# A gated mix of linear attention and a Mish layer on one core: more products by blocks, a packed 96-unit tile, and a new order of all steps

## The chip, the core and the metric

The kernel runs on one core of a Trainium2 chip. Its time is the device time in microseconds of a launch; a profile of one execution gives the span from its first to its last instruction. Engines: TensorE (PE; PEld is its weight load), VectorE (DVE), ScalarE (ACT), GpSimd (POOL) and SyncE (SP), which issues most transfers.

## The reference

All in float32. x has 2048 rows of 512; there are 32 heads of 16.

```python
qkv = (x @ wqkv)                                    # q, k, v: 32 heads of 16
pq, pk = q @ w_phi, k @ w_phi                       # per head, 16 x 16
phi_q = concat(softmax(pq), softmax(-pq))           # 32 features a head; phi_k likewise
kv, z = sum_s phi_k^T v, sum_s phi_k                # over all 2048 rows
o = (phi_q kv) / (phi_q z + 1e-6)
a = o @ wo                                          # 512 x 512
h = x @ w1 + b1                                     # 512 x 1376
b = (h * tanh(softplus(h))) @ w2                    # Mish, 1376 x 512
g = sigmoid(sum(x * gate_w))
out = g * a + (1 - g) * b
```

## The kernel before

**Number format.** Almost every product is made of fp32r matmuls of 128 rows by 128 columns by 512. Each operand is split into a high part (a copy rounded to fp32r, on ScalarE) and a low part (operand minus high part, on VectorE or GpSimd). A product is then three matmuls: high by high, high by low, low by high. In the names a last letter h or l is the high or low part (wkh, wkl, xh, xl).

**Start.** The per-head w_phi is laid out as block-diagonal tiles `bds` and multiplied into the key and query weights once ("fuse"): for the keys by `fuse`, 128x128 matmuls, one bank per row tile k of the weights; for the queries by `fuse_tiles`, which sets 64x64 matmuls on four corners of the array, two row tiles a call. The result is copied out (raw: wkr, wqr) and split (wkh, wkl, wqh, wql).

**Part A: 8 chunks of 256 rows.** A chunk makes keys k, queries q and values v for its two row tiles: `proj`, 12 matmuls each (3 parts by 4 row tiles of the weights). Chunks 2 to 5 (`FAST`) make keys and queries with seven block products instead of eight: `fast_ops` has s1 to s7, six matmuls each; bc, m7, ca and qa carry partial results between banks; `fast_operands` makes sums of blocks of x (sa) and splits them (sh, sl); `tops` makes the sums of weight blocks. Keys go through maximum, minimum (mx, mn), two differences (d0, d1), Exp (E), sums (S), reciprocals (rS) and a scaling (ml). kv multiplies feature maps and values; z adds the maps up over chunks (in memory for the first chunks, then in a tile). The queries are stored to memory (`pqd`).

**Part B: 4 blocks of 512 rows.** The hidden layer has 11 unit tiles. The tile that holds the last 96 units of the first 736 also holds the gate's column, and comes first. up makes a tile (12 matmuls), mi applies Mish, hi and lo split it, dn adds its product to the four output banks (12 matmuls: three for each row tile t). Beside this the queries are loaded (lq) and go the same way as the keys; T, D, m, de, rd, sc, es multiply by z, form the denominator and scale; tr transposes 32x32 squares; mv moves the squares into place by 16 transfers for two row tiles; nu multiplies by kv; oh, ol split; wo multiplies by wo; ag, fi mix with the gate and store the block.

**Order.** Every instruction keeps its place in program order on its engine. The order is written out by hand: one text for each chunk and block (FIRST to LAST, BLOCK0 to BLOCK), whose words name steps. A mark ' is the chunk before, + the one after, # a step on the weights: L loads a piece of w1 or w2, H and O split it (O on GpSimd, with an added dependency that puts it behind a VectorE step, `behind`). All pieces are loaded and split during part A. Buffers come in turn from pools: PSUM has 3 banks "a", 4 banks "dn" (output and scratch) and 1 bank "kv".

Of the kernel before, what the change touches and what calls it, by code (L numbers as in the profile page):

```python
# [39 lines left out]
FIRST = """  # L40
    fq v0 fh0 fh1 wr0 wr1 fh2 fh3 fl0 fl1 wr2 wr3 mx0 mn0 d00 d10 fl2 fl3 xh xl ldx ve0 E0 mx1 mn1 d01 d11 v1 t1# t3# t4# ve1 E1
    S0 rS0 ml0 S1 rS1 ml1 q0 qe0 st0 q1 qe1 st1
"""
SECOND = """
    L0# L1# h0# h1# sa ldx z0' z1' k0 mx0 mn0 d00 d10 k1 E0 xh mx1 mn1 d01 d11 v0 E1 S0 rS0 ve0 sh0 ml0 xl sl0 z0
    v1 S1 rS1 ml1 ve1 q0 qe0 st0 q1 qe1 st1 t2# sh1
"""
THIRD = """
    h3# l1# h2# l2# l3# v0 kk ve0 H0# xh xl sl1' z1' l0# s1 bc sa s7 m7 H1# s2 mx0 mn0 s6 ca d00 d10 E0 ldx sh0 sl0 v1 O0# L2# ve1
    S0 s5 qa rS0 s4 st1 mx1 mn1 d01 d11 s3 qe0 st0 ml0 O1# L3# z0  # L50
"""
FOURTH = """
    s1 bc E1' S1' rS1' ml1' ve1' s7 m7 sh1' s2 xh s6 ca xl z1' sl1' sa ldx H2# O2# L4# mx0 mn0 d00 d10 E0 v0 ve0 sh0 sl0 H3#
    s4 s5 qa st1 S0 rS0 mx1 mn1 d01 d11 v1 s3 qe0 st0 ml0 z0
"""
SEVEN = """
    s1 bc E1' S1' rS1' ml1' ve1' s7 m7 sh1' s2 kk xh xl z1' early zld sa more mx0 s6 ca mn0 d00 d10 E0 ldx v0 ve0 sh0 sl0 za rest S0 rS0
    s4 s5 qa st1 mx1 mn1 d01 d11 E1 ml0 late v1 S1 rS1 s3 ve1 qe0 st0 ml1
"""
NEXT = """  # L60
    lq0+ k0 xh xl O8# L6# mx0 mn0 k1 kk d00 d10 ldx H9# E0 O9# ldw0 L10# z0' mx1 mn1 d01 d11 H6# E1 S0 rS0 ml0 z1' v0 ve0
    S1 rS1 ml1 O6# ldw1 v1 ve1 q0 mx0+ mn0+ d00+ d10+ z0 z1 qe0 st0 q1 qe1 st1 H10# O10# E0+ lq1+
"""
LAST = """
    k0 mx0 mn0 d00 d10 k1 E0 XH0 kv' mx1 mn1 d01 d11 E1 v0 S0 rS0 ml0 z0 ve0 ldo XH1 mx1+ mn1+ S1 rS1 ml1 d01+ d11+
    XL0 XL1 z1 v1 ve1 E1+ lq2+ q0 WH0 qe0 st0 q1 WH1 qe1 st1 tb kv S0+ rS0+ km zh0 zl0 zh1 zl1
"""

BLOCK0 = """
    up0 mi0 hi0 lo0 gr lq3 S1 rS1 mx2 mn2 d02 d12 up1 @z mi1 hi1 lo1 T0 D0 m0 de0 rd0 sc0 es0 tr0 up2 mi2 hi2 lo2 WL0 dn0
    T1 D1 m1 de1 rd1 sc1 es1 tr1 mv0 lq0+ lq1+ mx3 mn3 d03 d13 up3 @kt mi3 hi3 lo3 WL1 dn1
    up4 mi4 hi4 lo4 dn2 E2 S2 T2 rS2 D2 m2 de2 rd2 sc2 es2 tr2 up5 mi5 hi5 lo5 dn3 E3 ge gg up6 mi6 hi6 lo6 dn4
    up7 mi7 hi7 lo7 dn5 nu0 oh0 S3 T3 rS3 ol0 D3 m3 de3 rd3 sc3 es3 tr3 mv1 up8 mi8 hi8 lo8 dn6
    mx0+ mn0+ d00+ d10+ mx1+ mn1+ d01+ d11+ lq2+ lq3+ wo0 ag0 wo1 ag1 E0+ E1+ S0+ T0+ rS0+ D0+ m0+ de0+ rd0+ sc0+ es0+ tr0+
    up9 mi9 hi9 lo9 dn7 up10 mi10 hi10 lo10 dn8 S1+ T1+ nu1 oh1 ol1 rS1+ D1+ LX0 LX1 m1+ de1+ rd1+ sc1+ es1+ tr1+ mv0+
    XH0+ XL0+ XH1+ XL1+ dn9 wo2 ag2 wo3 ag3 df0 fi0 df1 fi1 df2 fi2 df3 fi3
"""
BLOCK1 = """  # L80
    up0 mi0 hi0 lo0 gr mx2 mn2 d02 d12 mx3 mn3 d03 d13 up1 mi1 hi1 lo1 E2 E3 S2 T2 rS2 D2 m2 de2 rd2 sc2 es2 tr2
    up2 mi2 hi2 lo2 dn0 nu0 oh0 ol0 S3 T3 rS3 D3 m3 de3 rd3 sc3 es3 tr3 lq0+ lq1+ mv1 up3 mi3 hi3 lo3 dn1 up4 mi4 hi4 lo4 dn2
    mx0+ mn0+ d00+ d10+ mx1+ mn1+ d01+ d11+ lq2+ lq3+ up5 mi5 hi5 lo5 dn3 E0+ E1+ ge gg wo0 ag0 wo1 ag1
    S0+ T0+ rS0+ D0+ m0+ de0+ rd0+ sc0+ es0+ tr0+ up6 mi6 hi6 lo6 dn4 up7 mi7 hi7 lo7 dn5 nu1 oh1 ol1 S1+ T1+ rS1+ D1+ LX0 LX1
    m1+ de1+ rd1+ sc1+ es1+ tr1+ mv0+ mx2+ mn2+ d02+ d12+ mx3+ mn3+ d03+ d13+ up8 mi8 hi8 lo8 dn6 E2+ E3+
    wo2 ag2 wo3 ag3 up9 mi9 hi9 lo9 dn7 up10 mi10 hi10 lo10 dn8 XH0+ XL0+ XH1+ XL1+ dn9 df0 fi0 df1 fi1 df2 fi2 df3 fi3
"""
BLOCK = """
    up0 mi0 hi0 lo0 gr S2 T2 rS2 D2 m2 de2 rd2 sc2 es2 tr2 up1 mi1 hi1 lo1 up2 mi2 hi2 lo2 dn0 nu0 oh0 ol0
    S3 T3 rS3 D3 m3 de3 rd3 sc3 es3 tr3 lq0+ lq1+ mv1 up3 mi3 hi3 lo3 dn1 up4 mi4 hi4 lo4 dn2  # L90
    mx0+ mn0+ d00+ d10+ mx1+ mn1+ d01+ d11+ lq2+ lq3+ up5 mi5 hi5 lo5 dn3 E0+ E1+ ge gg wo0 ag0 wo1 ag1
    S0+ T0+ rS0+ D0+ m0+ de0+ rd0+ sc0+ es0+ tr0+ up6 mi6 hi6 lo6 dn4 nu1 oh1 ol1 S1+ T1+ rS1+ D1+ LX0 LX1 m1+ de1+ rd1+ sc1+
    es1+ tr1+ mv0+ up7 mi7 hi7 lo7 dn5 mx2+ mn2+ d02+ d12+ mx3+ mn3+ d03+ d13+ up8 mi8 hi8 lo8 dn6 E2+ E3+
    wo2 ag2 wo3 ag3 up9 mi9 hi9 lo9 dn7 up10 mi10 hi10 lo10 dn8 XH0+ XL0+ XH1+ XL1+ dn9 df0 fi0 df1 fi1 df2 fi2 df3 fi3
# [4 lines left out]
def tile_gated_mix(ctx: ExitStack, tc: tile.TileContext, xT, wv, wkT, wqT, bd, w1a, w1b, b1, w2a, w2b, wo, out):  # L99
# [100 lines left out]
    ge_sb = const.tile([P, S // P], F32, name="ge_sb")  # L200
# [17 lines left out]
    xs, Es, vs, psA, low = {}, {}, {}, {}, {}  # L218
# [38 lines left out]
    def x_lo(c, j, eng):  # L257
        low[c] = dve[0] = pin(eng.tensor_sub(xs[c][1][j], kt(rawx[c], SC)[:, 2 * j : 2 * j + 2, :], f32(xs[c][0][j])))

    def feat_ops(key, t, src, d, negative=False):  # L260

        n = str(t)

        def red(name, op):
            d[name] = T([P, H], F32, name, 2, name)
            pin(V.tensor_reduce(d[name], hv(src()), axis=AX.X, op=op))
# [12 lines left out]
        def ss():
            d["S"] = T([P, 2 * H], F32, "Sm", 2, "Sm")  # L280
            pin(V.tensor_reduce(d["S"], hv(d["E"][:, :]), axis=AX.X, op=ALU.add))  # L281
# [7 lines left out]
        at(key, "rS" + n, lambda: pin(V.reciprocal(d["S"], d["S"])))

    dve = {}

    def behind(ins, other=None):
        tc.add_manual_dep(ins.ins, (other or dve[0]).ins.name, SYNC, reason="VectorE's step first")

    def scale_by(d, eng):
        dve[0] = pin(eng.tensor_mul(hv(d["E"][:, :]), hv(d["E"][:, :]), d["S"][:, :, None].to_broadcast([P, 2 * H, DH])))  # L297

# [32 lines left out]
    def fast_operands(c, key):  # L331
# [12 lines left out]
        for j in range(2):  # L344
# [615 lines left out]
```

## Time and profile before

| | |
|---|---|
| median of 3 runs | 447.27 us (447.27 to 448.22) |
| span of the profiled execution | 446.1 us |
| TensorE busy | 439.7 us, 99% |
| VectorE busy | 319.6 us, 72% |
| ScalarE busy | 211.3 us, 47% |
| GpSimd busy | 158.9 us, 36% |
| transfers | 46.35 MB, mean 104 GB/s |

The profiled execution's own launch time is not listed; its span is 1.17 us under the median. A busy bar of a matmul overlaps that of the next, so the busy share of TensorE is not its rate: the rate is read from the distance between starts. L111 is the helper that records every matmul, so groups are told apart by their tiles (up, down, proj, num, kvp, wo, fuse).

### The profile page before, as it was taken

What the parts mean: (1) busy time and instruction counts of PE and PEld (TensorE: products, weight loads), DVE (VectorE), ACT (ScalarE), POOL (GpSimd) and SP (SyncE); (2) the same over time, 40 slices, a digit from 0 to 9 for tenths busy, and PEclk for the clock granted to TensorE, in tenths of its full rate; (3) what the DMA queues carried; (4) which work ended last, traced back from release to release, by engine and by line L of the source; (5) the groups of instructions that cost most, each with busy time, mean ns of one, the idle gap of its engine ahead of it and who ended that gap; (6) DMA issues with size and microseconds to landing.
All of it is one profiled execution on the core that took longest, in us unless ns stands there. A gap on an engine that the chain in (4) does not pass through costs nothing.

```text
span 446.1 us, 7022 instructions
## 1 busy us (share of the span) xinstructions
PE 439.7 (99%) x2748; PEld 359.1 (81%) x2748; DVE 319.6 (72%) x427; ACT 211.3 (47%) x292; POOL 158.9 (36%) x120
## 2 busy tenths in 40 slices
PE   7999999999999999999999999999999999999996
PEld 7888888788888888787878887887887888787885
DVE  2499789888999999799899868386967438701002
ACT  5774644463544837426374443724253544234220
POOL 2297388675666364212023121113202123121211
PEclk9999999999999999999999999999999999999999
DMA  7424559949835111405251241321241302030002
GB/s 281 169 77 160 143 122 233 220 130 312 240 116 166 49 24 32 112 19 148 89 171 49 55 134 48 94 96 47 49 143 48 94 2 95 1 91 5 0 0 94
DMA packets 27320, 46.35 MB, mean 104 GB/s; under 512 B 5908, under 2 KB 14100, under 8 KB 27288
## 3 DMA queue, kind: packets, MB, share of 16 engines
q1 hardware_dynamic: 25528, 39.88, 28.9%
q0 software_dynamic: 1616, 5.77, 6.5%
q8 instruction: 21, 0.34, 0.3%
q10 hardware_dynamic: 144, 0.26, 0.2%
q14 instruction: 11, 0.09, 0.1%
HBM read 23.87 MB, written 13.64 MB: 84 GB/s over the span
## 4 chain that ended last, share of the span: by engine, by line
PE 98%; DMA 1%; DVE 0%; issue 0%
PE proj L111 28%; PE up L111 27%; PE down L111 27%; PE wo L111 10%; PE num L111 2%; PE fuse L111 2%; PE kvp L111 2%; DMA bds<-in_bd_dram 1%; DVE io L797 0%; PE z L111 0%; PE kvT L616 0%
## 5 line engine op out<-in xcount | busy, mean ns | idle before, releaser
L662 POOL TENSOR_TENSOR l<-act,h 128x512 fp32r<-128x512 f32 x44 | 60.4, 1373 | 220.5 <-ACT h L131 184.7
L131 ACT ACTIVATE act<-up,b1s 128x512 f32<-128x512 f32 x44 | 30.3, 689 | 87.4 <-PE up L111 87.3
L131 ACT ACTIVATE E<-E 128x1024 f32<-128x1024 f32 x32 | 33.7, 1060 | 47.9 <-DVE E L275 33.8
L297 DVE TENSOR_TENSOR E<-E,Sm 128x1024 f32<-128x1024 f32 x32 | 42.2, 1320 | 1.0
L281 DVE TENSOR_REDUCE Sm<-E 128x64 f32<-128x1024 f32 x32 | 38.7, 1210 | 4.2 <-ACT E L131 4.2
L111 PE MATMUL wo<-woh,ohl 128*128 128x512 f32 x128 | 40.7, 389 | 0.0
L111 PE MATMUL down<-w2ah,h 128*128 128x512 f32 x96 | 37.5, 390 | 0.0
L111 PE MATMUL down<-w2ah,l 128*128 128x512 f32 x96 | 37.4, 389 | 0.0
L111 PE MATMUL down<-w2al,h 128*128 128x512 f32 x96 | 37.3, 389 | 0.0
L797 DVE SCALAR_TENSOR_TENSOR io<-down,og_sb,io 128x512 f32<-128x512 f32 x16 | 11.1, 748 | 31.0 <-PE down L111 31.0
L111 PE MATMUL down<-w2bh,h 128*128 128x512 f32 x80 | 31.2, 390 | 0.0
L111 PE MATMUL down<-w2bl,h 128*128 128x512 f32 x80 | 31.1, 389 | 0.0
L111 PE MATMUL down<-w2bh,l 128*128 128x512 f32 x80 | 31.1, 389 | 0.0
L131 ACT ACT_TABLE_LOAD x20 | 25.7, 1283 | 10.1 <-PE up L111 9.8
L771 DVE TENSOR_TENSOR ohl<-num,ohl 128x512 fp32r<-128x512 f32 x16 | 10.2, 678 | 26.4 <-ACT ohl L131 26.4
L131 ACT ACTIVATE h<-act 128x512 fp32r<-128x512 f32 x44 | 27.8, 632 | 1.4
L111 PEld LDWEIGHTS wo<-woh,ohl 128*128 128x128 f32 x128 | 24.0, 188 | 5.0
L111 PE MATMUL up<-xbh,w1ah 128*128 128x512 f32 x96 | 26.2, 394 | 0.0
L111 PE MATMUL up<-xbh,w1al 128*128 128x512 f32 x96 | 25.7, 389 | 0.0
L111 PE MATMUL up<-xbl,w1ah 128*128 128x512 f32 x96 | 25.7, 389 | 0.0
L559 DVE TENSOR_TENSOR xbl<-xraw,xbh 128x1024 fp32r<-128x1024 f32 x8 | 10.1, 1290 | 21.0 <-ACT xbh L131 21.0
L111 PE MATMUL wo<-wol,ohl 128*128 128x512 f32 x64 | 24.9, 389 | 0.0
(155 smaller groups left out, 1015.3 us busy)
## 6 DMA issues: line engine op xcount, KB each, us to landing
xraw<-in_xT_dram SPq DMA_DIRECT2D x16, 512.0 KB, 4.6
eT<-tt SPq DMA_DIRECT2D x128, 64.0 KB, 2.0
zd<-E POOLq DMA_DIRECT2D x10, 512.0 KB, 7.4
pqd<-qs SPq DMA_DIRECT2D x16, 256.0 KB, 4.0
pq<-pqd SPq DMA_DIRECT2D x16, 256.0 KB, 2.9
out_dram<-io SPq DMA_DIRECT2D x16, 256.0 KB, 2.1
raw<-in_w1a_dram SPq DMA_DIRECT2D x3, 512.0 KB, 4.2
raw<-in_w2a_dram SPq DMA_DIRECT2D x3, 512.0 KB, 3.6
```

Source lines behind the costliest of these rows:

```text
L111: return pin(nc.tensor.matmul(*a, **k))
L131: return pin(A_.activation(out_, in_, fn, **k))
L281: pin(V.tensor_reduce(d["S"], hv(d["E"][:, :]), axis=AX.X, op=ALU.add))
L297: dve[0] = pin(eng.tensor_mul(hv(d["E"][:, :]), hv(d["E"][:, :]), d["S"][:, :, None].to_broadcast([P, 2 * H, DH])))
L559: dve[0] = pin(V.tensor_sub(xb[b][1][:, :, sl], kt(raw[h], SC), f32(xb[b][0][:, :, sl])))
L662: pin(G_.tensor_sub(U[i]["l"], U[i]["a"], f32(U[i]["h"])))
L771: pin(V.tensor_sub(ohl[h, gp][:, 512:], num[h, gp], f32(ohl[h, gp][:, :512])))
L797: pin(V.scalar_tensor_tensor(io[t], dn[t], og_sb[:, i : i + 1], io[t], op0=ALU.mult, op1=ALU.add))
```

## The change

1. `FAST` is chunks 2 to 7: chunks 6 and 7 make keys and queries by seven block products too.
2. The key weights are fused by `fuse_tiles` as well; `fuse` is gone.
3. The first unit tile (96 units) has its low parts put into its 32 free rows: two matmuls for each row tile instead of three, and a step dc of four matmuls over 32 rows for the remaining 32 units' low parts. w2 gets matching rows (`w2_moves`, six transfers on GpSimd's queue).
4. The second parts of w1 and w2 (pieces 4, 5, 9, 10, 11) are loaded and split in the first block of part B.
5. Transposed feature maps go through memory: a store (st) and four loads (ld) for each row tile; the transpose is in place. In part B the reciprocals rS are gone: the sums of the other half are multiplied in instead.
6. One text `ORDER` of 44 lines replaces the texts for chunks and blocks. A word is a step; `A3:` names its chunk; `@` gives the buffer or bank by number; a last v or g puts the step on VectorE or GpSimd; `^` adds the dependency on the last VectorE step noted. dn steps are single row tiles (a to d).

```diff
-FAST = range(2, 6)
+FAST = range(2, 8)
+SUM = 5
...
+ORDER = """
+    P0| lk0 lk1 fk0@12 lx0@0 kh1 kl1 lk2 kh0 kl0 xh0 kr1 lk3 fk1@30 kr3 kr2 kr0 kh2 xl0v kl2 lx1 xh1 xl1g kh3 lq2 lq3 p00@0 p01@1 p10 fq1@21 qh3 p11 kl3 p21 p31 A0:mx1@0
+    P0| A0:d01@0 lq1 A0:mn1@0 A0:d11 ldx@1 A0:xh@4576 A0:xl1g^ qr2 qr3 p20 p30 A0:mx0@1 A0:mn0@1 A0:d10@1 A0:xl0g qh2 ql2 lq0 A0:E1 lv0@0 vh0 vl0g fq0@30 lv1@1 A0:ldx@0
...
+    A7| s6 ca@0 B0:LX0@1 B0:XH0 mx0@1 A6:rS0 B0:LX1@0 B0:lq0@1 v1@1 ve1@0 B0:XL0v A6:rS1 d10@2 s5 A6:ml1v s4 B0:XH1 B0:XL1v mn1@1 W:L3@0 W:H3 qa W:wm A6:v0@3 st1 d00
+    A7| v0@0 A6:ve0@1 mx1@0 E0 d11@3 d01 E1 S0@0 rS0 B0:up0@1 B0:mi0@4 B0:ha@5 s3 A6:ml0g^ A6:z0g qe0@0 A6:v1@1 st0 S1@1 ml0g^ rS1 B0:mx0@1 A6:ve1@2 B0:d00g@1 ve0@3
+    B0| A6:z1v A7:z0v A7:ml1v A7:z1v A7:zh0@10 up2@2 mi2@7 mn0@0 A6:kv A7:kv A7:km@1 hb@6 pi d10v up3@0 W:L4@1 A7:zl0v ph W:H4 W:O4v up1@2 dn0d@3 lq2@0 mi3@0 A7:zh1
+    B0| A7:zl1g mn2@1 A7:z0b@2 E0 d12g@0 dn0a@1 W:O3v lq1@1 mn1@0 A7:zc0 A7:z1b@0 h3@2 up4@0 l3g^@1 dn0b@2 mi1@3 mx2@0 W:L5@1 W:H5 W:O5g up7@2 up10@1 A7:zc1 dn0c@0
...
+    B0| dn2a lq3@1 S0@0 m0 dn2d de0 rd0 sc0 mn3@1 d13g^@3 E2 dn2c mi5@4 up6@0 S1@1 m1 de1 rd1 mx3@1 d03g^ B1:lq0@0 sc1 es0v tr0 es1v W:L9@1 tr1 dn2b B1:lq1@1 st0 up8@2
+    B0| T2g@0 st1 D2@0 S2@0 mi7@7 W:H10 W:O10g^ m2 h5@2 l5g@1 dn4b dn5b up9@0 de2 W:L11@0 B1:mx1@0 W:H9 W:O9g mi6@3 h6@0 rd2 mi10@4 sc2 dn5d l6v@5 dn6d E3 T3v@0 dn6abc
+    B0| dn5ac W:H11 h7@6 l7g@3 ld0 dc es2g^ A7:kc ld1 mi8@7 h8@0 W:O11v l8g@5 nu0@1 dn8b mi9@2 dn8c B1:mn0@0 dn8d B1:mn1@1 A7:ldo@1 h9@1 l9g@7 dn9cd S3@1 B1:XH0 dn9b
...
-    def fuse(staged, k):
-        acc = psum("fuse", "dn")
-        for G in range(NG):
-            mm(acc[:, G * P : (G + 1) * P], staged[:, k, G, :], bds[:, G, :], start=(G == 0), stop=(G == NG - 1), skip_group_check=True)
-        return acc
...
+        def down_mm(t, a, w):
+            n = left.setdefault(t, 3 * NF)
+            if n == 3 * NF:
+                dn[t] = psum("down", "dn")
+            left[t] -= 1
+            mm(dn[t], a, w, start=(n == 3 * NF), stop=(n == 1), skip_group_check=True)
 
         def down(i, t):
...
-            for n, (a, x) in enumerate(((h, 0), (h, 1), (l, 0))):
-                mm(dn[t], a, w2_tile(f, x), start=(i == 0 and n == 0), stop=(i == NF - 1 and n == 2))
+            for a, x in (("h", 0), ("h", 1), ("l", 0)) if i else (("h", 0), ("i", 1)):
+                down_mm(t, U[i][a][:, t * P : (t + 1) * P], w2_tile(UNITS[i], x))
+
+        def ha(x):
+            U[0][x] = k2("h", "hl", F32R)
+            act(U[0][x][:REST, :], U[0]["a"][:REST, :])
+
+        def mo(x):
+            u = U[0]
+            if x == "c":
+                u["c"] = T([P, P], F32R, "lc", 1, "lc")
+            for t in range(4) if x == "c" else (None,):
+                o, sl = {"h": 0, "i": 32, "c": 64}[x], slice(None) if t is None else slice(t * P, (t + 1) * P)
+                dst = u[x][REST:, :] if t is None else u["c"][32 * t : 32 * t + 32, :]
+                vv(V.tensor_sub(dst, u["a"][o : o + 32, sl], f32(u["h"][o : o + 32, sl])))
+
+        def dc():
+            for t in range(4):
+                o = slice(32 * t, 32 * t + 32)
+                down_mm(t, U[0]["c"][o, :], wc[o, :])
...
+            def st(d=d, i=i):
+                eTd[i] = tc.dram_tile([P, 1024], F32, name=f"eTd{i}")
+                pin(Sy.dma_start(eTd[i][:, :], d["E"]))
+
+            def ld(t=t, i=i):
...
+                src = eTd[i].rearrange("(q i) (k x) -> k i q x", q=4, k=4)
+                for k in range(4):
+                    o = 64 * (k % 2) + 32 * (k // 2)
+                    pin(Sy.dma_start(eTs[h][o : o + 32, t % 2, :, :], src[k]))
...
-    run(FIRST, ("A", 0))
...
+    run(ORDER)
```

At the start the steps are: lk, lq load a row tile of the key or query weights, lx, lv halves of x and of the value weights; fk0, fk1, fq0, fq1 are the calls of `fuse_tiles`; kh, kl, kr (qh, ql, qr) copy and split a fused half; xh0, xl0, xh1, xl1 split chunk 0's x; p00 to p31 (row tile k of the weights, row tile t) are chunk 0's key products, three matmuls each. hb and ph, pi, pc fill the free rows of the 96-unit tile.

More of the change, by code (lines that the diff above doesn't have):

```diff
@@ L31 @@
 NF = NFA + NFB
-GROW = FA % P
-ORDER = [NFA - 1] + list(range(NFA - 1)) + list(range(NFA, NF))
+GROW = REST = FA % P
 WARM = 6
-FAST = range(2, 6)
[L40 to L94, printed above, removed]
+FAST = range(2, 8)
@@ L814, in tile_gated_mix @@
         b_ops(b)
-    acc = {}
-    def fsplit(h, l, k):
-        act(h[:, k, :], acc[k])
-        pin(V.tensor_sub(l[:, k, :], acc[k], f32(h[:, k, :])))
+    acc, pk = {}, {}
     new_x(0)
-    pk = {}
-    def k_part(k):
-        for t in range(2):
-            sl = slice(t * P, (t + 1) * P)
-            if t not in pk:
-                pk[t] = psum("proj", "a")
-            for n, (a, w) in enumerate(((xs[0][0], wkh), (xs[0][0], wkl), (xs[0][1], wkh))):
-                mm(pk[t], a[k // 2][:, k % 2, sl], w[:, k, :], start=(k == 0 and n == 0), stop=(k == KT - 1 and n == 2))
@@ L895, in tile_gated_mix, with k_part @@
-    for c, text in ((NCH - 2, NEXT), (NCH - 1, LAST)):
-        run(text, ("A", c), ("A", c - 1), ("B", 0))
-    for b in range(NB):
-        run((BLOCK0, BLOCK1, BLOCK, BLOCK)[b], ("B", b), ("B", b - 1), ("B", b + 1))
+    def k_part(k, t):
+        if not k:
+            pk[t] = psA[0]["k", t] = psum("proj", "a")
+        for n, (a, w) in enumerate(((xs[0][0], wkh), (xs[0][0], wkl), (xs[0][1], wkh))):
+            mm(pk[t], a[k // 2][:, k % 2, t * P : (t + 1) * P], w[:, k, :], start=(k == 0 and n == 0), stop=(k == KT - 1 and n == 2))
@@ new lines, in tile_gated_mix, with ps @@
+    for n, wh, wl, wr in (("k", wkh, wkl, wkr), ("q", wqh, wql, wqr)):
+        for i in range(4):
+            h, l, r = [w[:, i // 2 * 2 : i // 2 * 2 + 2, :].rearrange("p k (g r f) -> p r (k g) f", r=2, f=64)[:, i % 2, :, :] for w in (wh, wl, wr)]
+            def ps(n=n, i=i):
+                return acc[n, i][:, :].rearrange("p (g f) -> p g f", f=64)
+            at(PRE, f"{n}h{i}", lambda h=h, ps=ps: act(h, ps()))
+            at(PRE, f"{n}r{i}", lambda r=r, ps=ps: act(r, ps()))
+            at(PRE, f"{n}l{i}", lambda h=h, l=l, ps=ps: pin(V.tensor_sub(l, ps(), f32(h))))
```

515 lines of the change are left out of this document (277 added, 238 removed).

## The prediction

> **What bounds the kernel now.** I read the page's busy times first, then its chain of waits, then the waits of TensorE alone, and last the timeline where TensorE is not yet or no longer saturated.
>
> ```profile
> span 446.1 us, 7022 instructions
> PE 439.7 (99%) x2748; PEld 359.1 (81%) x2748; DVE 319.6 (72%) x427; ACT 211.3 (47%) x292; POOL 158.9 (36%) x120
> PE 98%; DMA 1%; DVE 0%; issue 0%
> PE fuse L111 <- DMA bds<-in_bd_dram: 1.4, 1, 1.4
> PE warm L111 <- DVE ones L179: 1.1, 1, 1.1
> ```
>
> TensorE is the chain: 98% of it, and its only two listed waits are in the first 5.5 us. A busy 99% could hide slack, since a matmul's bar (389 ns) overlaps the next, so I take the pitch from the chain's pieces:
>
> ```profile
> 157.05 2.72 PE down L111 x12
> 159.77 2.72 PE up L111 x12
> ```
>
> Twelve 128x512 matmuls advance the chain by 2.72 us: 0.227 us each. Of 2748 records, 944 are small (256 num, 512 kvp, 160 fuse, 12 warm, 4 kvT); the other 1804 are such matmuls, 409 us at that pitch. So every one taken out is worth 0.227 us as long as nothing else becomes late.
>
> The start and the end:
>
> ```profile
> 5.48 4.91 PE L111 MATMUL fuse<-bds,wT 128*128 128x128 f32 x24 [1.43 <-DMA bds<-in_bd_dram]
> 7.59 0.60 ACT L131 ACTIVATE wkh<-fuse 128x512 fp32r<-128x512 f32 x1 [3.45 <-PE fuse L111]
> 8.09 1.14 ACT L131 ACTIVATE xh<-xraw 128x512 fp32r<-128x512 f32 x2
> 8.23 0.69 DVE L821 TENSOR_TENSOR wkl<-fuse,wkh 128x512 fp32r<-128x512 f32 x1 [7.16 <-ACT wkh L131]
> 10.15 0.48 PE L111 MATMUL proj<-wkh,xh 128*128 128x512 f32 x1
> 11.61 1.05 PE L111 MATMUL fuse<-bds,wT 128*128 128x128 f32 x8
> 12.41 0.48 PE L111 MATMUL proj<-wkh,xh 128*128 128x512 f32 x1
> L258 POOL TENSOR_TENSOR xl<-xraw,xh 128x512 fp32r<-128x512 f32 x2 | 2.5, 1292 | 3.8 <-ACT xh L131 3.8
> 13.19 1.08 ACT L131 ACTIVATE wkr<-fuse 128x512 f32<-128x512 f32 x2
> 16.68 2.11 PE L111 MATMUL fuse<-bds,wT 64*64 64x64 f32 x128
> 18.73 1.19 PE L111 MATMUL proj<-wvh,xh 128*128 128x512 f32 x4
> 440.27 2.85 DVE L797 SCALAR_TENSOR_TENSOR io<-down,og_sb,io 128x512 f32<-128x512 f32 x4 [28.85 <-PE down L111]
> 441.88 0.39 PE L111 MATMUL down<-w2bh,l 128*128 128x512 f32 x1
> ```
>
> By 18.73 us both fuses and chunk 0's keys are done. The last matmul is issued at 441.88; 4 us of evacuation and output remain.
>
> From 18.73 to 442.11 are 423.4 us. The work there is 1780 matmuls (403.5), 8 num groups, 8 kvp groups and the transposes (0.6). The two small groups cost this much:
>
> ```profile
> 146.66 1.10 PE L111 MATMUL kvp<-E,v 128*32 128x64 f32 x64
> 147.69 1.20 PE L111 MATMUL up<-xbh,w1ah 128*128 128x512 f32 x4
> 187.08 0.39 PE L111 MATMUL down<-w2ah,l 128*128 128x512 f32 x1
> 187.40 1.09 PE L111 MATMUL num<-eT,kvb 64*32 64x256 f32 x32
> 188.42 1.20 PE L111 MATMUL up<-xbh,w1bh 128*128 128x512 f32 x4
> ```
>
> A kvp group takes 147.69 - 146.66 = 1.03 us; a num group 188.42 - (187.08 + 0.23) = 1.11. Together 403.5 + 8.9 + 8.2 + 0.6 = 421.2: the middle loses only 2.2 us of 423.4. The change cannot win by removing waits; it wins by removing matmuls, or loses by adding waits.
>
> **The change, part by part.**
>
> *Chunks 6 and 7 by block products.* Four projections for keys and queries are 48 matmuls, seven products of six are 42. Two chunks: 12 fewer, 12 x 0.227 = **-2.72 us** of TensorE.
>
> *The 96-unit tile.* Per block and row tile the first unit's down product falls from three matmuls to two: 4 x 0.227 = 0.907 us less per block. The step dc comes in: four matmuls of 32 rows by 128 columns, 512 long, each on its own quarter of the rows and into its own bank. No run here shows that shape. Nearest is num, on 64x32 tiles. Eight fuse records of 128 columns advance TensorE by 12.41 - 11.61 = 0.80, 0.10 each, so 256 columns are 0.2. One after another num's 32 would be 6.4 us, beside each other on four column groups only 1.6, on all eight tiles 0.8. It took 1.11, so row halves do run together, and some 0.31 is left for the change of shape. For dc that gives 0.227 + 0.31 = 0.54 beside each other, 0.907 + 0.31 = 1.22 in turn; 0.23 if the change were free. I take 0.54, since num showed the overlap: 4 x (0.54 - 0.907) = **-1.5 us** (ends -2.7 and +1.25).
>
> The Trainium skill (TensorEngine Tiling (Array Packing), Tiling Modes) says that changing the tiling mode drains TensorE; num's 0.31 agrees. The skill (TensorE: Matmul & The Clock Gate, Part 3) gives 3.07x for four row tiles of this size; by that dc would be an estimated 0.295 us and the term -2.4.
>
> *Both fuses in 64x64 and the new start.* The queries' fuse, already in 64x64, takes 18.73 - 16.68 = 2.05 us for two calls, 1.03 each; the keys' costs 0.80 for each of four. But the start is a chain through ScalarE, so I follow it. The first 24 fuse records took 10.15 - 5.48 = 4.67 us, 0.195 each against 0.10 later, so at the start a call costs 2.05: fk0 ends at 7.53, when the first fuse ends now (wkh starts at 7.59). Then fk1 follows at the same half rate until 9.6, while ScalarE does kh1, kh0, xh0 (0.60, 0.60, 0.57) until 9.36. p00 starts at 9.6, not 10.15. p00, p01, p10 end at 11.6; ScalarE has four copies kr (0.55 each, wkr's row) until 11.56, which free fq1's banks; fq1 and p11 end at 13.35. kh2, xh1, kh3 end at 13.33; kl3 on VectorE (0.69) and xl1 on GpSimd (1.29 after xh1 at 12.73) at 14.05. So p21 loses 0.45 and ends at 14.5; p31, p20, p30, fq0 end at 17.6, where 18.73 stands now: **-1.1 us**. Its ends: -2.0 if fk1 is at full rate and ScalarE is never waited for; +1.2 by the third rival. The next step, chunk 1's keys, has its input split by then: ScalarE reaches it after qh3, at 15.3.
>
> *Second parts of w1 and w2 split in the first block.* No TensorE work. The tight spot is up7, which needs all of the second part of w1. Its last piece may be loaded only when O4 has freed the buffer:
>
> ```profile
> raw<-in_w2b_dram SPq DMA_DIRECT2D x1, 256.0 KB, 2.9
> L131 ACT ACTIVATE w1bh<-raw 128x512 fp32r<-128x512 f32 x1 | 0.6, 635 | 0.4 <-DMA raw<-in_w1b_dram 0.4
> L526 POOL TENSOR_TENSOR w1bl<-raw,w1bh 128x512 fp32r<-128x512 f32 x1 | 1.3, 1297 | 1.2 <-ACT E L131 1.2
> ```
>
> The chain is 2.9 + 0.64 + 1.30 = 4.8 us; on TensorE up1, dn0d, z0b, dn0a, z1b, up4, dn0b stand between, 2 x 2.72 + 5 x 0.45 = 7.7. Hidden, with 2.9 to spare; without that cover it would cost up to 4.8 once.
>
> *Feature maps through DRAM.* Per row tile one store of 512 KB and four loads of 128 KB replace eight moves of 64 KB. Nearest rows:
>
> ```profile
> xraw<-in_xT_dram SPq DMA_DIRECT2D x16, 512.0 KB, 4.6
> eT<-tt SPq DMA_DIRECT2D x128, 64.0 KB, 2.0
> raw<-in_wo_dram SPq DMA_DIRECT2D x8, 128.0 KB, 2.9
> ```
>
> So 4.6 + 2.9 = 7.5 us instead of about 2. On SP ld waits for the store, with the loads lq, LX and W behind it. Between st1 and nu0 of the first block stand nine down steps (0.68), up9 and dc, 9.4 us: hidden with 1.9 to spare. Uncovered it costs at most 7.5 - 2.0 = 5.5 for a group.
>
> *Load of the others.*
>
> ```profile
> L131 ACT ACT_TABLE_LOAD x20 | 25.7, 1283 | 10.1 <-PE up L111 9.8
> 18.73:147.76 129.03, 129.03 (x1046) 106.00 (x1041) 116.58 (x151) 71.05 (x102) 85.00 (x59) 1.00 0.60 166
> 118.06:147.76 29.70, 29.70 (x249) 24.25 (x249) 28.80 (x36) 14.67 (x18) 19.37 (x9) 1.00 0.43 143
> L281 DVE TENSOR_REDUCE Sm<-E 128x64 f32<-128x1024 f32 x32 | 38.7, 1210 | 4.2 <-ACT E L131 4.2
> L289 DVE RECIPROCAL Sm<-Sm 128x64 f32<-128x64 f32 x32 | 17.6, 549 | 0.6
> L297 DVE TENSOR_TENSOR E<-E,Sm 128x1024 f32<-128x1024 f32 x32 | 42.2, 1320 | 1.0
> L266 DVE TENSOR_REDUCE mx<-proj 128x32 f32<-128x512 f32 x16 | 10.9, 679 | 2.9 <-PE proj L111 2.8
> L320 DVE TENSOR_TENSOR w2al<-wqr,w2ah 128x1024 fp32r<-128x1024 f32 x2 | 2.4, 1224 | 0.8 <-ACT w2ah L131 0.8
> ```
>
> VectorE loses the reciprocals of the feature sums in the blocks; part of its scaling and subtracting goes to GpSimd. Exp and Mish alternate more: I count 32 changes of table in the order against 20 loads now, 12 x 1.283 = 15.4 us on ScalarE, which is at 47%; at no place in front of TensorE by itself. What is dense is VectorE while the chunks run.
>
> Now 116.58 of 129.03 us are VectorE's (the third of the busy times in these two rows of a table by stretches, after TensorE's two), 90.4%, and 28.80 of 29.70, 97%, in the last stretch, with TensorE never waiting. In the new order, its fourth to seventeenth line (chunk 1's queries to the first block's up1) hold for TensorE 42 terms (1.36), 16 projections and 4 up (2.72), 8 kvp groups and a dn0: 120.2 us. For VectorE: 82 half-tile steps of 0.68 (maxima, minima, differences, ca, qa, low parts; the mx row), 15 sums of 1.21 and 15 reciprocals of 0.55, 9 scalings of 1.32, and what is given to it of weight splits, operand sums and the z sums, worth 20 steps of 1.22 (the w2al row). 55.8 + 18.2 + 8.2 + 11.9 + 24.4 = 118.5 us, 98.6% of TensorE's. VectorE can run ahead and lag (the next two lines have 11.4 for 21.2), so I take no stall beyond the 2.2 us the middle loses now. Ends: -2.2, nothing lost; +10.9 by the first rival.
>
> *Sum.* 446.1 - 2.7 - 1.5 - 1.1 + 0 = 440.8 us span. The median of 447.27 lies 1.17 above the profiled span, so **442.0 us**.
>
> **The rivals.**
>
> *VectorE becomes the bound in chunks 2 to 7 (slower).* If it keeps only the 90.4% it has now over the chunks, its 118.5 us need 131.1, and TensorE waits 10.9: 452.9 us. For it: 98.6%, and in-order steps that wait for ScalarE (the 4.2 us in the Sm row). Against: 97% over 30 us without a TensorE wait. The gain is gone when it keeps less than 118.5 / (120.2 + 5.3) = 94%.
>
> *The quarters run in turn.* The change then does not do what it says: dc 1.22, +2.7, 444.7 us. Against it is num's 1.11.
>
> *The start stays at half rate longer.* For the 4.67 us of those 24 records TensorE ran at half its later pitch, though the profile's granted clock prints 1.00 for it. In the new start it waits for ScalarE at more places; another such stretch costs half of itself, 2.3: 444.3 us. Against it: my start has no gap on TensorE over 0.5 us.
>
> The Trainium skill (TensorE: Matmul & The Clock Gate, Part 1) says that the clock is halved after an idle window of about 3.4 us; by that rule this rival needs a gap several times as long as any in my start.
>
> **How the numbers follow.** Forecast 0.66; VectorE 0.18; quarters 0.08; start 0.08. A change under 0.3% (1.3 us) can't be told from none here. Forecast, quarters and start are all faster, 0.82. Of VectorE's 0.18 I give 0.06 to a stall of 4 to 6.6 us, which ends within 0.3%, and 0.12 to more. The range begins at 442.0 - 2.2 - 1.2 = 438.6 (no loss in the middle, dc at its cheap end) and reaches into VectorE's case, to 5.5 us of stall: 447.5. The forecast's own range is 438.6 to 444.
>
> **What would show it.** 1776 large matmuls and 16 dc records instead of 1804; a dc group that advances TensorE by about 0.5 us; chunk 1's keys starting near 17.6 us; no TensorE wait over 1 us in the middle. Wrong, if TensorE's waits name VectorE (mx, ca, l, ml) in the chunks, or eT or w1b in the first block.

## The result, and the profile after

The changed kernel takes **450.25 us** (449.37 to 450.65, 4 runs) against 447.40 of the kernel before beside it: 1.0054 times as long, interval [1.0040, 1.0069]. Slower by over 0.3%, and above the range, which ended at 447.5. The profiled execution took 450.02 us, its span is 448.3 against 446.1.

From the page of the kernel after, the span, the busy times and the chain's shares by engine:

```profile
span 448.3 us, 7210 instructions
PE 439.9 (98%) x2832; PEld 353.5 (79%) x2832; DVE 327.4 (73%) x433; ACT 227.9 (51%) x312; POOL 187.4 (42%) x139
PE 83%; DVE 13%; DMA 1%; issue 1%; SPq 0%; ACT 0%; DVEq 0%
```

TensorE is busy 439.9 us, as before (439.7), although there are fewer large matmuls: 2832 records less 512 kvp, 256 num, 256 fuse, 16 dc, 12 warm and 4 kvT are 1776, as predicted. So those that are left must have become longer, or waits hide in the busy time. The waits of TensorE:

```profile
PE fuse L128 <- DMA bds<-in_bd_dram: 1.4, 1, 1.4
PE warm L128 <- DVE ones L185: 1.1, 1, 1.1
PE fuse L128 <- DMA w1ahf<-in_wkT_dram: 1.1, 2, 0.6
PE wo L128 <- DVE wol L618: 0.4, 1, 0.4
```

Nothing from VectorE in the chunks; 1.5 us are new, most of it at the start. (The chain runs over VectorE for 13% of the span, but it does so in the faster e5 below as well, and TensorE's waits name VectorE for the 0.4 us alone.) The pieces of the chain show the rest (start, length, twelve matmuls each):

```profile
243.23 2.80 PE up L128 x12
270.69 2.73 PE down L128 x12
277.61 2.72 PE wo L128 x12
```

Before, twelve of up's matmuls advanced the chain by 2.72 us; now they take 2.80, 233 ns each instead of 227. Shape, type and count of these matmuls are the same; the granted clock is full in both. There are 528 of them.

To see how much that is, I summed for every matmul the time from its start to the next one's start, by output, from the records. The sums go from the first projection behind both fuses to the last matmul. That projection is chunk 1's keys in the kernel after and chunk 0's values in the kernel before, where the twelve projections more are the saved ones. The third column belongs to the experiment e5 below:

```
                           before    after    e5 (distance 0)
first projection            18.73    19.64    19.98
down, with dc              120.45   119.62   118.94
proj                       121.13   118.87   118.23
up                         120.73   123.56   120.18
wo                          43.54    44.91    44.87
kvp, num, z, kvT            17.28    17.17    17.15
last matmul to the end       4.22     4.55     4.55
sum                        446.1    448.3    443.9
```

Three things ate the gain: every kind of large matmul except wo is 0.6 to 3.4 us dearer than in e5; wo lost 1.4; the start lost 0.9 instead of winning 1.1.

### The profile page after: what moved, and what is told of

It reads as the page before. It is cut to its first block, busy times and chain, and to the rows that moved or that the text cites. A ratio compares the mean times of both kernels' runs of the same rounds, so it can differ in the third digit from the quotient of the medians.

```text
span 448.3 us, 7210 instructions
## 1 busy us (share of the span) xinstructions
PE 439.9 (98%) x2832; PEld 353.5 (79%) x2832; DVE 327.4 (73%) x433; ACT 227.9 (51%) x312; POOL 187.4 (42%) x139
## 4 chain that ended last, share of the span: by engine, by line
PE 83%; DVE 13%; DMA 1%; issue 1%; SPq 0%; ACT 0%; DVEq 0%
PE proj L128 26%; PE up L128 22%; PE down L128 21%; PE wo L128 10%; PE kvp L128 2%; DVE E L330 2%; PE num L128 2%; DMA w1ahf<-in_wkT_dram 1%; DVE Sm L314 1%; DVE Dn L781 1%; DVE den L791 1%; PE fuse L128 1%; DVE E L819 1%; DVE T L777 1%; DVE mn L300 1%
## 5 line engine op out<-in xcount | busy, mean ns | idle before, releaser
L702 POOL TENSOR_TENSOR l<-act,h 128x512 fp32r<-128x512 f32 x27 | 36.7, 1359 | 99.4 <-ACT h L155 87.5
L128 PE MATMUL wo<-woh,ohl 128*128 128x512 f32 x128 | 41.9, 391 | 0.1
L155 ACT ACTIVATE h<-act 128x512 fp32r<-128x512 f32 (+1 forms) x48 | 30.1, 630 | 20.5 <-PE down L128 9.5
L128 PE MATMUL down<-w2ah,l 128*128 128x512 f32 x80 | 31.3, 391 | 0.0
L702 DVE TENSOR_TENSOR l<-act,h 128x512 fp32r<-128x512 f32 x13 | 11.0, 844 | 25.8 <-PE down L128 10.4
L819 DVE STREAM_TRANSPOSE E<-E 128x1024 f32<-128x1024 f32 x16 | 19.9, 1244 | 9.5 <-POOL E L330 9.1
L128 PE MATMUL up<-xbh,w1ahr 128*128 128x512 f32 x96 | 26.5, 398 | 0.0
L777 POOL TENSOR_TENSOR T<-E,zb 128x1024 f32<-128x1024 f32 x7 | 18.1, 2586 | 20.0 <-ACT E L155 20.0
L128 PE MATMUL up<-xbh,w1alr 128*128 128x512 f32 x96 | 26.3, 395 | 0.0
L128 PE MATMUL up<-xbl,w1ahr 128*128 128x512 f32 x96 | 26.3, 395 | 0.0
```

Source lines behind the costliest of these rows:

```text
L128: return pin(nc.tensor.matmul(*a, **k))
L155: return pin(A_.activation(out_, in_, fn, **k))
L702: on_(e)(e.tensor_sub(U[i]["l"], U[i]["a"], f32(U[i]["h"])))
L777: on_(e)(e.tensor_mul(d["T"], d["E"], B["zb"]))
L819: at(key, f"tr{t}", lambda d=d: pin(V.transpose(d["E"][:, :], d["E"][:, :])))
```

## What differs about up's matmuls

Shape, type and count being the same, I looked at the places of the operands: the stationary one (128x128, which PEld loads) and the moving one (128x512). The change removed ge_sb (64 bytes per partition), and moved w1's parts from the pool to a fixed block ahead of the constants. Byte addresses per partition, from the layouts of the two kernels:

```
             stationary w1a   stationary w1b    moving xbh    (xbh - w1) mod 256
before           20352        118656, 128896       69504              0
after            36992         16512               71488            192
```

The first theory, called A: matmuls take longer where both operands no longer stand at the same place of a 128-byte line as before. When e1 to e3 had spoken against it, its successor, A2: the distance between the moving and the stationary operand, modulo 256 bytes, decides. The rival of both: the pitch has nothing to do with addresses but with the busier neighbours, VectorE, ScalarE and GpSimd.

## Experiments

Beside these runs the kernel before took 447.80 to 447.99 us.

**e1: 64 bytes put in front (distance 128).**

```
+    g_sb = nc.alloc_sbuf_tensor("g_sb", [P, S // P], F32)   # ahead of the arena
-    g_sb = const.tile([P, S // P], F32, name="g_sb")
```

> The changed kernel with one edit: the 64-byte tile g_sb lies in front of w1 instead of behind it, so that w1 starts at 64 bytes modulo 128 like every other operand (in the changed kernel w1 is at 0, all others at 64; in the kernel before all are at 0). No step moves. Theory A, the address phase of the two operands: up's pitch goes back from 233 to 227 ns, some 540 matmuls with mixed phases gain 6.6 ns each, 3.6 us: 446.6 us. Theory B, SBUF traffic of the other engines and more transfers stretch the matmuls: pitch stays, 450.2 us. Theory C, only the start is late and the rest is a measure of clock: no change, 450.2 us.

Measured 450.57, 1.0060 [1.0046, 1.0074]. Theory A falls. The chain of e1:

```profile
243.72 2.80 PE up L129 x12
```

**e2: the kernel before, with 64 unused bytes behind w1a (distance 64 for w1a alone).**

```
+    T([P, 16], F32, "pad", 1, "pad")     # behind w1a
```

> The kernel before with an unused 64-byte tile allocated right behind the first part of w1, so that this part stays at 0 modulo 128 and everything allocated after it in that pool is at 64. No step moves. Theory A: the 288 up matmuls of the first six unit tiles (w1a at 0, xbh and xbl at 64) go from 227 to 233 ns, 1.9 us: 449.3 us; those of w1b stay at 227. Theories B and C: 447.4 us.

Measured 448.15, 1.0007 [0.9997, 1.0017]: no change that can be told. The chain shows an effect of less than half the size, on w1a's units alone (the first of these rows; the second is a unit of w1b):

```profile
154.53 2.75 PE up L111 x12
176.90 2.72 PE up L111 x12
```

So an address does act, in a kernel with no other change, but 64 bytes cost 2 ns per matmul and not 6.

**e3: the kernel after, everything behind the arena moved by 32 bytes (distance 224).**

```
+    pad = const.tile([P, 8], F32, name="pad")
```

> The changed kernel with 32 more bytes in front of the other operands: w1 at 0, all others at 96 modulo 128. Theory A in its coarse form (operands need the same position in a 128-byte line): up stays near 233 ns, 450.2 us. Theory A in its fine form (only an odd multiple of 64 between them costs): up near 227 ns, 446.6 us. Theories B and C: 450.2 us with up at 233 ns.

Measured 450.73, 1.0067 [1.0054, 1.0081]; up stays slow, twelve take 2.79 us, so the fine form falls too:

```profile
302.82 2.79 PE up L128 x12
```

**e4: e1 with a longer warm-up.** Four more warm matmuls (`WARM = 10`), to take the start off half rate.

> e1 with ten warm-up matmuls instead of six (20 records at 0.22 us, so TensorE is busy until about 5.5 us, when the first weights land). Theory: TensorE ran at half rate until 12.4 us because of its gaps (3.75 to 5.46, 6.6 to 7.05, 8.2 to 8.79); with the first gap filled, fk1 takes 1.0 instead of 2.0 us and p00, p01 run at 0.227: chunk 1's keys start 1.5 us earlier and the time is 1.5 us under e1. Rival: the start is set by the landing of the weights and by ScalarE's copies: 0.5 us or less under e1.

Measured 450.19, 1.0052 [1.0039, 1.0065], against e1's 1.0060: the same within the intervals. The timeline of e4's start:

```profile
8.79 1.28 PE L129 MATMUL fuse<-bds,w1ahf 64*64 64x64 f32 x64 [1.05 <-DMA w1ahf<-in_wkT_dram]
10.00 0.50 PE L129 MATMUL proj<-wkh,xh 128*128 128x512 f32 x1
10.34 0.39 PE L129 MATMUL proj<-wkl,xh 128*128 128x512 f32 x1
13.36 0.50 PE L129 MATMUL proj<-wkh,xh 128*128 128x512 f32 x1
15.16 0.39 PE L129 MATMUL proj<-wkl,xh 128*128 128x512 f32 x1 [1.30 <-issue]
```

TensorE did run at full rate here (64 fuse records in 1.28 us, projections 0.23 apart), and then stood 1.3 us behind the first matmul of p11. What it waited for is open: the profile names no engine (issue), and the splits in flight there, on VectorE and GpSimd, had ended by 14.1. Chunk 1's keys start at 19.52. What the faster rate gave, the wait took.

**e5: the kernel after with distance 0.** 192 bytes of small constants are placed in front of the arena instead of behind it; not one instruction is added or moved.

```
+    g_sb, og_sb = [nc.alloc_sbuf_tensor(n, [P, S // P], F32) for n in ("g_sb", "og_sb")]
+    b1s = nc.alloc_sbuf_tensor("b1s", [P, NF], F32)      # both ahead of the arena
-    b1s, g_sb, og_sb as const.tile(...)
```

> The changed kernel with g_sb, og_sb and b1s (192 bytes together) in front of w1, so that the distance from every stationary to every moving operand of the large matmuls is a multiple of 256 bytes, as in the kernel before. No step moves. Theory A2 (what counts is that distance modulo 256: before 0, 227 ns; e2's shifted part 64, 229; e1 128, 233; the changed kernel 192, 233; e3 224, 233): all of up at 227 ns, 560 matmuls gain 6.5 ns: 446.6 us. Theory B (traffic of the other engines): up stays at 231 to 233 ns, 450.3 us.

Measured **445.86**, 0.9954 [0.9936, 0.9971]: 4.4 us below the kernel after, and below the kernel before. The chain:

```profile
241.42 2.72 PE up L130 x12
```

**e6: the kernel before with distance 192 for w1a.** The counter-proof: 192 unused bytes behind w1a, nothing else.

```
+    T([P, 48], F32, "pad", 1, "pad")     # behind w1a
```

> The kernel before with 192 unused bytes behind the first part of w1: its distance to xbh and xbl is then 192 modulo 256, as in the changed kernel. No step moves. Theory A2: the 288 up matmuls of w1a at 233 ns, those of w1b at 227: 1.9 us more, 449.8 us where the kernel before takes 447.9. Theory B: all stay at 227, 447.9 us.

Measured 449.95, 1.0049 [1.0034, 1.0063], 1.96 us above the kernel before. The chain, two units of w1a and then one of w1b, whose distance stayed 0:

```profile
153.72 2.80 PE up L111 x12
159.25 2.80 PE up L111 x12
176.37 2.72 PE up L111 x12
```

Inside one execution the part whose distance was changed is slow and the other is not, with the same neighbours beside both; that rival falls. By distance the runs give for up: 0, 227 ns; 64, 229; 128, 192 and 224, 233. In the kernel after, down has some operand pairs 256 bytes apart (256 modulo 512), and these stay at 227 to 228, so the period is 256.

Two things this rule leaves open. In the kernel after, 48 matmuls of the block products stand at distance 64 too, and not at 229: 30 of them take 235 to 237 ns and 17 take 226 or 227, nearly all of the latter in front of a matmul whose stationary operand has distance 0 to the same moving one. So what is loaded for the next matmul may count as well; that was not tested. And all of down's pairs are at 0 modulo 256, yet down lost 0.7 us in the table. Why the chip does this no run here shows.

**e7: e5 with the 96-unit tile in three products.** The packed product dc and the copies that feed it go out, the third 96-row product comes back.

```
-            for a, x in (("h", 0), ("h", 1), ("l", 0)) if i else (("h", 0), ("i", 1)):
+            for a, x in (("h", 0), ("h", 1), ("l", 0)):
-        at(key, "dc", dc)
```

> e5 with the 96-unit tile in three products for each row tile as before: no dc, no filling of free rows, no moves of w2. Theory: the packed form is worth what its matmuls say, 16 taken out at 0.227 us and 16 quarter ones in at 0.109: 1.9 us more than e5. Rival: the low parts put into the free rows (VectorE, in front of the down products) hold TensorE up, and packing is worth less than 1 us.

Measured 447.81, 0.9997 [0.9984, 1.0009], 1.95 above e5. In the sums of the two profiles down differs by 1.92 (120.86 against 118.94). The packing is worth what its matmuls say.

**e8: e5 with its waits mended.** Ten warm matmuls, the start's steps reordered (the keys' roundings ahead of the raw copies, the queries' fuse behind chunk 0's keys), and wo's split issued ahead of the feature scaling es3.

```
-  ... kl0 xh0 kr1 lk3 fk1@30 kr3 kr2 kr0 kh2 ... p10 fq1@21 qh3 p11 kl3 p21 p31 ...
+  ... kl0 xh0 lk3 fk1@30 xl0v kh2 ... kh3 kl3 ... p10 p11 p21 p31 kr1 kr0 kr3 kr2 ... p20 p30 fq1@21 ...
-  ... A7:WH0 es3v tr3 st3 ge dn9a WL0v oh0@10 ...
+  ... A7:WH0 WL0v es3v tr3 st3 ge dn9a oh0@10 ...
```

> e5 with three more edits: ten warm-up matmuls; at the start ScalarE splits all of the keys' weights (kh2, kh3) before it makes the raw copies, and the queries' first fuse stands behind chunk 0's keys; WL0, the split that wo waits for, stands in front of es3 on VectorE. Theory: chunk 1's keys start at 17.5 instead of 19.6 us, and wo loses nothing at 205 us: 3 us under e5, 443.7 us. Rival: what is gained at the start is waited for at chunk 1, whose VectorE steps end no earlier: 1 us under e5.

Measured **443.59**, 0.9908 [0.9889, 0.9927]: it beats both kernels. But its profiled execution, 445.36 us, was the slowest of its six, and chunk 1's keys started at 19.41 there, not at the 17.5 expected. The timeline of e8, and the window behind it (span, then the engines in the order TensorE, its loads, VectorE, ScalarE, GpSimd; then the granted clock):

```profile
5.69 0.72 PE L130 MATMUL fuse<-bds,w1ahf 64*64 64x64 f32 x32
7.63 0.69 PE L130 MATMUL fuse<-bds,w1ahf 64*64 64x64 f32 x32 [1.22 <-DMA w1ahf<-in_wkT_dram]
9.08 1.93 PE L130 MATMUL fuse<-bds,w1ahf 64*64 64x64 f32 x64 [0.76 <-DMA w1ahf<-in_wkT_dram]
```

```profile
8.50:12.40 3.90, 3.32 (x68) 2.91 (x69) 2.58 (x4) 2.87 (x6) 0.19 (x1) 0.59 1.05 391
```

TensorE began at full rate (32 fuse records in 0.72 us), waited twice for wkT, 1.22 and 0.76 us, and fell back to half rate (64 in 1.93), which here the granted clock shows: 0.59. So this execution doesn't tell what the edits at the start are worth. The edit for wo won nothing in it: wo's sum is 44.91, in e5 44.87. The median is what the theory said, but not by the way it said; e10 and e11 take the edits apart.

**e9: e5 with chunks 6 and 7 in four projections.**

```
+PLAIN = (6, 7)      # s1, s2: first keys; ca, s4: second keys; s6, s3: first queries; s7: second queries
```

> Chunks 6 and 7 go back to four projections for keys and queries (48 matmuls each instead of 42), on the kernel with distance 0; their operand sums, the copy that frees the partial keys, and the two combining steps on VectorE are left out, everything else stays. Theory (a matmul taken out is worth its pitch, nothing else is late): 12 more matmuls, +2.7 us against the 445.9 us of distance 0, 448.6 us, 1788 large matmuls, and VectorE busy some 10 us less without any gain from it. Rival (the denser VectorE of the block products cost TensorE waits): under +1.5 us, below 447.4 us, and the time from chunk 6's first matmul to the first block's up0 grows by less than 2 us.

Measured 449.86, 1.0048 [1.0035, 1.0060], 4.0 above e5 and not 2.7. From chunk 1's keys to the last matmul the sums per output differ from e5's at two places only: proj + 2.72, exactly twelve matmuls, and up + 1.24. Most of the latter is two waits for one piece of w1, for its high and then its low part (timeline of e9):

```profile
164.93 0.63 ACT L158 ACTIVATE w1bhr<-raw 128x512 fp32r<-128x512 f32 x1 [0.34 <-DMA raw<-in_w1b_dram]
165.61 0.19 PEld L131 LDWEIGHTS up<-xbh,w1bhr 128*128 128x128 f32 x1 [0.44 <-ACT w1bhr L158]
165.64 1.62 POOL L574 TENSOR_TENSOR w1blr<-raw,w1bhr 128x512 fp32r<-128x512 f32 x1
167.32 0.50 PE L131 MATMUL up<-xbh,w1blr 128*128 128x512 f32 x1 [0.51 <-POOL w1blr L574]
```

The last piece of w1's second part came late for up7. Its load waits for O4, the split that frees its buffer: O4 ended at 156.28 us in e5 and at 161.66 in e9, 5.4 us later behind 2.7 us of matmuls; 1.0 of that is O4 itself, which took 2.26 us beside a step of GpSimd, not 1.22. The rival, that the denser VectorE cost waits, is wrong: with less work for VectorE (323.5 us busy against 325.2) the kernel got slower by more than its matmuls, and the projections by exactly theirs.

**e10: e5 with wo's split ahead of es3 alone.** The second pair of e8's diff lines.

> Distance 0, and in the first block the split of wo's first half on VectorE is issued ahead of the feature scaling es3 instead of behind it. Theory (the 0.9 us wait of TensorE for wo's split is VectorE's queue order): the wait goes, 445.0 us against 445.9. Rival (es3 is slow because GpSimd splits wo's other half at the same time, so whichever of the two stands last is late): the wait stays or moves to a matmul that reads the scaled features or to the later half, 445.9 us.

Measured 446.30, 0.9951 [0.9934, 0.9968]: as e5. The rival was right: the wait moved. VectorE's timeline in the kernel after, and GpSimd's beside it:

```profile
200.37 3.30 DVE L330 TENSOR_TENSOR E<-E,Dn 128x1024 f32<-128x1024 f32 x1
204.87 1.18 DVE L618 TENSOR_TENSOR wol<-raw,woh 128x1024 fp32r<-128x1024 f32 x1
200.17 2.42 POOL L618 TENSOR_TENSOR wol<-raw,woh 128x1024 fp32r<-128x1024 f32 x1 [0.53 <-ACT woh L155]
```

And in e10, with the two steps of VectorE exchanged:

```profile
198.02 2.60 DVE L617 TENSOR_TENSOR wol<-raw,woh 128x1024 fp32r<-128x1024 f32 x1 [0.74 <-ACT woh L157]
200.54 1.21 DVE L329 TENSOR_TENSOR E<-E,Dn 128x1024 f32<-128x1024 f32 x1
197.12 2.42 POOL L617 TENSOR_TENSOR wol<-raw,woh 128x1024 fp32r<-128x1024 f32 x1 [0.54 <-ACT woh L157]
203.66 0.50 PE L130 MATMUL wo<-woh,ohl 128*128 128x512 f32 x1 [0.74 <-DVE ohl L842]
```

Whichever stands beside GpSimd's 2.42 us is stretched (es3 1.21 to 3.30, the split 1.18 to 2.60), and TensorE loses 0.9 us to what comes last, now ohl, by the distances between wo's starts (the idle time shown is less, since a bar overlaps the next start). To win this, GpSimd's half must go elsewhere; that was not tried.

**e11: e5 with the start alone** (the warm-up and the first pair of e8's diff lines).

> Distance 0, ten instead of six warming matmuls and the start reordered alone (the third and fourth rounding of the keys' weights ahead of the raw copies on ScalarE, the queries' fuse behind all of chunk 0's keys), without the earlier split of wo. Theory (the 2.3 us that the mended kernel's median lies below distance 0 come from the start): 443.6 to 444.5 us, and chunk 1's keys start 1.5 to 2 us earlier than in the runs with the start as changed (19.6 to 20.0 us). Rival (the start's time is set by when TensorE leaves half rate, which the order does not steer): 445.5 us or more, chunk 1's keys no earlier than 19.2 us.

Measured 444.66, 0.9932 [0.9912, 0.9953]; in its profiled execution TensorE stayed at full rate (64 fuse records in 1.28 us from 8.21, projections 0.23 apart) and chunk 1's keys start at 17.23. In the profile the theory holds; the median lies between its range and the rival's. The interval meets those of e5 and e8, so how much of e8's 2.3 us is the start and how much chance is not settled. One part of the scatter shows: in e11 the three executions with a mean granted clock of 0.998 or more took 443.00 to 443.98 us and the three at 0.992 to 0.995 took 445.33 to 446.40; in e10 the five at 0.992 took 446.30 to 446.69 and the four at 0.998 or more 443.88 to 445.87. The last fuse and the next step, in e5, in e10 (which has e5's start, step for step), and in e11:

```profile
18.89 1.16 PE L130 MATMUL fuse<-bds,w1alf 64*64 64x64 f32 x64
19.98 1.19 PE L130 MATMUL proj<-wkh,xh 128*128 128x512 f32 x4
```

```profile
17.09 1.16 PE L130 MATMUL fuse<-bds,w1alf 64*64 64x64 f32 x64
18.18 1.19 PE L130 MATMUL proj<-wkh,xh 128*128 128x512 f32 x4
```

```profile
16.30 1.00 PE L130 MATMUL fuse<-bds,w1alf 64*64 64x64 f32 x56
17.23 1.20 PE L130 MATMUL proj<-wkh,xh 128*128 128x512 f32 x4
```

e5 and e10 differ by 1.8 us at the same place of the same start: in e5 the nine matmuls from 10.09 to 14 stood 0.43 apart, in e10 0.23. The order alone doesn't set the start; when TensorE leaves half rate differs from execution to execution, and a single profile can't tell a start's worth to better than that.

## Why the prediction was wrong, step by step

**The step that failed: "every one taken out is worth 0.227 us as long as nothing else becomes late".** That holds for what is taken out (e9: 2.72 us for twelve), but I took the pitch of the 1776 that stay for granted. The kernel after runs 4.8 us longer than e5 between chunk 1's keys and the last matmul, 3.4 of it in up, by nothing but the operands' places; the medians say 4.4. My own signs of being wrong missed it: no wait names VectorE in the chunks, and none names eT or w1b; of the signs of being right only the start failed. No part of my working looked at where tiles lie, though the diff removes a tile and fixes two others, and the trace of before could not have warned of it, as all its matmuls had distance 0. The range had no room for it: its upper end was VectorE's case.

**The start: -1.1 predicted, +0.9 measured.** The timeline of the kernel after:

```profile
5.46 1.13 PE L128 MATMUL fuse<-bds,w1ahf 64*64 64x64 f32 x32 [1.40 <-DMA bds<-in_bd_dram]
7.05 1.13 PE L128 MATMUL fuse<-bds,w1ahf 64*64 64x64 f32 x32 [0.46 <-DMA w1ahf<-in_wkT_dram]
8.79 1.98 PE L128 MATMUL fuse<-bds,w1ahf 64*64 64x64 f32 x64 [0.61 <-DMA w1ahf<-in_wkT_dram]
10.71 0.79 PE L128 MATMUL proj<-wkh,xh 128*128 128x512 f32 x1
11.30 0.63 PE L128 MATMUL proj<-wkl,xh 128*128 128x512 f32 x1
12.81 0.40 PE L128 MATMUL proj<-wkh,xl 128*128 128x512 f32 x1
19.64 1.19 PE L128 MATMUL proj<-wkh,xh 128*128 128x512 f32 x4
```

My chain ran through ScalarE and had no transfers in it: "fk1 follows at the same half rate until 9.6". But fk0 waits in its middle for the second part of wkT, and fk1 for the rest until 8.79, so p00 starts at 10.71, 1.1 us late. Then TensorE stays at half rate until about 12.5 (0.42 from one projection to the next, later 0.23), while the granted clock prints 1.00:

```profile
8.50:12.40 3.90, 3.61 (x68) 3.20 (x69) 1.89 (x3) 3.37 (x8) 0.00 (x0) 1.00 1.04 397
```

Four projections take 1.86 us there instead of 0.91, 0.95 more. So the rival that I gave 0.08 did strike, but for 0.95 us; the other 1.1 are transfers, which no rival had. That the two together, 2.0 us (19.64 against 17.6), come near the 2.3 that I had reckoned for it is luck. With the same start e10 has 18.18, and e11 with its own 17.23. By itself this would have left the kernel faster.

Nor can the +0.9 be put down to the change from one execution of each kernel. In e2 and e6 the start of the kernel before is unchanged, and its first projection behind the fuses stands at 19.16 and 17.98, against 18.73.

My objection, that half rate needs a longer gap on TensorE than the start has, failed twice: here full rate merely came late, and in e8 it was lost after gaps of 1.2 and 0.8 us, which the 3.4 us idle window of the Trainium skill (TensorE: Matmul & The Clock Gate, Part 1) does not cover. What the same part says under What's actually happening, that the window runs freely and its phase differs from run to run, agrees with the 1.8 us between e5 and e10. The 500 ns that it gives for the spread are too little here: full rate came at 10.1 us in e10 and at 14.0 in e5.

**The 96-unit tile: -1.5 predicted, -1.9 measured.** The mechanism was right and dc at 0.54 a little dear. The timeline of the kernel after, one dc group and the next step, whose starts lie 0.44 apart:

```profile
196.96 0.51 PE L128 MATMUL down<-wc,lc 32*128 32x512 f32 x4
197.40 1.09 PE L128 MATMUL num<-eT,kvb 64*32 64x256 f32 x32
```

So the quarters do run beside each other, that rival is out, and 4 x (0.44 - 0.907) is -1.9 us, as e7 has it. That down's sum fell by 1.5 from before to e5, just as predicted, is partly chance: the first large matmul behind a small group takes 0.34 us instead of 0.23, and the new order put four more such places into down, 0.4 us, and took five out of up. The 3.07x of the Trainium skill (TensorE: Matmul & The Clock Gate, Part 3) was too good here: 0.907 to 0.44, which holds the change of shape, is 2.1x; my row for num, with 0.54, erred the other way.

**VectorE as the bound (0.18): not seen.** The window of the chunks in the kernel after (span of the window, then TensorE, its loads, VectorE, ScalarE, GpSimd):

```profile
19.64:147.76 128.12, 127.98 (x921) 104.88 (x916) 119.43 (x152) 68.34 (x99) 81.17 (x63) 1.00 0.53 147
```

VectorE keeps 93.2% of the stretch, more than the 90.4% it had, and TensorE loses nothing to it. The estimate of 118.5 us of work was near, though not for quite the same stretch; "can run ahead and lag" was the right reading.

**w1's and w2's second parts: hidden, but with less to spare.** In the kernel after the last split of w1's second part ends at 163.87 and the matmul that needs it starts near 164.3:

```profile
162.48 1.39 POOL L549 TENSOR_TENSOR w1blr<-raw,w1bhr 128x512 fp32r<-128x512 f32 x1 [1.24 <-ACT w1bhr L155]
163.64 1.09 PE L128 MATMUL up<-xbh,w1blr 128*128 128x512 f32 x4
```

That is under 0.5 us where I had reckoned 2.9, and in e9 the cover was gone (1.24 us). The feature maps' way through DRAM stayed hidden: 3.0 us for the store and 3.0 for a load, against my 4.6 and 2.9.

```profile
eTd<-E SPq DMA_DIRECT2D x16, 512.0 KB, 3.0
eT<-eTd SPq DMA_DIRECT2D x64, 128.0 KB, 3.0
```

**What I had not seen at all:** the 0.9 us wait in the first block's wo, and 0.3 between the last matmul and the end. The first is VectorE beside GpSimd (e10); the second was not tried. The other 0.4 that wo lost are again first matmuls behind small groups and last ones in front of them.

**The sum, term by term, on the profiled spans.** Projections -2.9 (predicted -2.7), the 96-unit tile -1.9 (-1.5), start +0.9 (-1.1), operand places +4.8 (0), wo's wait +0.9 (0), the rest of the middle +0.1 (0), end +0.3 (0): +2.2, from 446.1 to 448.3. The places are read from the kernel after against e5, the tile from dc's 0.44 and e7, the start from the kernel after, and the rest from e5 against the kernel before.

## What to carry to other kernels

When a change adds, drops or fixes a tile, write down the addresses of the operands of the most frequent matmuls before and after; here 64 bytes less and a new block cost more than the saved products won, and 192 bytes moved brought it back. Compare the length of an unchanged group of matmuls first (here 2.72 against 2.80 for twelve): a TensorE that is 98 to 99% busy in both profiles hides a change of pitch. And follow a start through its transfers too, and read it from more than one execution.

## What was not expected of the hardware

- The pitch of 128x512 matmuls depends on the distance between moving and stationary operand modulo 256 bytes: for up 227 ns at 0, 229 at 64, 233 at 128 to 224 (e1 to e6). At 64 it isn't one value: in the block products of the kernel after it is 235 to 237 or 226 to 227.
- A step of VectorE with two inputs stood almost as long as GpSimd's step overlapped it: 3.30 us instead of 1.21, 2.60 instead of 1.18. The Trainium skill (SBUF — State Buffer, SBUF: two separate sides) states this as a lock that one of the two holds for a whole instruction; the rows agree.
- TensorE's full rate came, by the distances between starts, at about 6.8 us (e11), 10.1 (e10), 12.5 (the kernel after) and 14.0 us (e5) into the execution. In e8 it was there by 5.8 us, lost at about 9.2 and back at 12.6. Where it had not yet come, the granted clock prints 1.00; where it was lost again (e8), 0.59.
